# Linear attention and a max-out layer on one core: the k and v projection of batches 3 to 7 moves to the first group spot, into a bank of the down layer

## The chip, the cores and the metric

The kernel runs on one core of one Trainium2 chip. The metric is the device time of one execution, in microseconds (us). Before the change four executions took 328.84, 328.88, 328.73 and 328.17 us, median 328.79. Inside the core five engines run side by side, each in the order of its own instructions: TensorE (PE; its weight loads are listed as PEld), VectorE (DVE), ScalarE (ACT), GpSimd (POOL) and SyncE (SP, which here only issues transfers). They wait for each other with semaphores. PSUM, the memory into which TensorE writes, has eight banks of 512 fp32 columns; what a bank holds must be copied out by VectorE or ScalarE before the bank takes something else.

## The reference

q, k and v are 8 batches x 8 heads x 1024 positions x 64. k and v are first projected from 1024 positions to 64 with E and F; attention over these 64 follows, then a layer of two up matrices, a maximum and a down matrix.

```python
k_proj = np.einsum('ks,bhsd->bhkd', E, k)
v_proj = np.einsum('ks,bhsd->bhkd', F, v)
scores = scale * np.matmul(q, k_proj.transpose(0, 1, 3, 2))
attn = softmax(scores)                       # over the 64 projected positions
x = np.matmul(attn, v_proj)                  # -> 8192 x 512
g = np.maximum(x @ w1, x @ w2)               # 512 -> 1024
out = g @ w_out                              # 1024 -> 512
```

The kernel uses max(a, b) = b + relu(a - b): it forms wd = w1 - w2 and m = w2 @ w_out, so that out = relu(x @ wd) @ w_out + x @ m. Operands are fp16, sums fp32.

## The kernel before

**Units.** The work behind the attention is cut into 16 units, two for each batch (unit n = 2 x batch + half). The up layer (x @ wd with the relu, `up_steps`, matmuls on line 558) and the down layer (`down_steps`, matmuls on line 636) of a unit are each done with seven products instead of eight (Strassen's scheme), from sums and differences of blocks that VectorE makes beforehand (`sums_x`, `sums_g`, line 519). The seven steps come in the order p1, p2, p6, p5, p7, p3, p4. An up step is four matmuls of 128x256, two times over for the two halves of the up layer; a down step is twelve matmuls, cut into three pieces of four.

**Slots.** The order of the work on TensorE is written out by hand in a list of slots. In unit n the down pieces of unit n alternate with the up steps of unit n + 1, and twice in a unit there is a group spot, the slot ("G", n, h). At the group spot the attention is carried on by one group (half the heads, a quarter of a batch): the score matmuls of the next group (line 266), and for the group before it the sums of the exponentials and the products with v (line 278). ScalarE then makes the exponentials (line 355), the logarithm of the sums (line 374) and its inverse (line 377), and VectorE multiplies (line 381). `at_slot` hangs further steps on a slot; they stand behind the slot's own work, in the order in which they were registered.

In an odd unit from 3 on, the first half is: two pieces of the down step p1, the group spot, the third piece of p1 and the first of p2, and then seven up steps with a down piece between each two. The second half has two pieces, the group spot, three pieces, and again seven up steps with pieces between.

**Banks.** Of the eight banks four (0 to 3) carry matmul results (`mm_bank`), and four are two attention tiles of two banks (`att_banks`, two buffers in turn). The up layer and the scores use banks 2 and 3; the down layer uses banks 0 and 1. In an odd unit the down step p1 is in bank 1 and the down step p2 in bank 0, its "second bank"; p6, p7 and p4 reuse the first and p5 and p3 the second. A down or up result that is needed later is copied out by ScalarE (`keep`, line 529); VectorE adds it to a later one (lines 573 and 660). In an even unit the banks 0 and 1 are exchanged, and its last step p4 leaves bank 0 through a ScalarE copy (line 704).

**The projection.** `step_kv` projects k and v of one batch: 8 pairs of matmuls of 512 columns (line 180), k into partitions 0 to 63 and v into 64 to 127 of one bank. For batches 3 to 7 it is hung on the second up step of unit n = 2 x batch - 3, ("U", n, 0, 1), and takes an attention tile. ScalarE copies k out (line 191). VectorE's part is in `finish_v`, which `step_kv` hands back and which is run one slot later: the copy of v (line 196), a doubling of k (line 198), the DMA transpose of k into kpt on SP's queue (line 223), and a copy of v to the other partitions (line 200). The scores of that batch begin at the second group spot of the same unit and need kpt. q of the batch is transposed by two DMAs on SP's queue, hung on the first group spot (line 249). Once kpt is there (`step_gate`, line 229), POOL issues the loads of the next batch's k, v and q.

Of the kernel before, what the change touches and what calls it, by code (L numbers as in the profile page):

```python
# [16 lines left out]
def kernel(  # L17
# [12 lines left out]
    nc = tc.nc  # L30

    B, H, S, D = q.shape
    KP = E.shape[0]
# [26 lines left out]
    def mm_bank(dtype=FP32, n=None):  # L60
        if n is None:
            n = turn.pop(0)
            turn.append(n)
        return ps.tile([128, 512 if dtype == FP32 else 1024], dtype, tag=f"mm{n}", name="mm_ps")

    def att_banks(dtype=FP32):
        return ps.tile(
            [128, 2, 512 if dtype == FP32 else 1024], dtype, tag="att", bufs=2, name="att_ps"
        )
# [53 lines left out]
    for f0, f1 in ((0, 256), (256, 512), (512, DF)):  # L123
        for w_sb, w in ((w2_sb, moe_w2), (w1_sb, moe_w1)):
            for z in range(2):
                nc.gpsimd.dma_start(
                    out=w_sb.rearrange("p (g z) f -> p g z f", z=2)[:, :, z, f0:f1],
                    in_=w.rearrange("(g p z) f -> p g z f", p=128, z=2)[:, :, z, f0:f1],
# [22 lines left out]
    for i in range(2):  # L151
        eft_ps = mm_bank()
        for c in range(NC):
            nc.tensor.transpose(
                out=eft_ps[:, c * KP : (c + 1) * KP],
                in_=ef_v[:, i, c, :],
# [3 lines left out]
        eng = nc.scalar.copy if i else nc.vector.tensor_copy  # L160
# [8 lines left out]
        t["qt"] = qtp.tile([128, H, HALF], FP16, tag="qt", name="qt_sb")  # L169


    def step_kv(t, h0=0, h1=H, which="kv", att=False, dma=False):
        kv_ps = att_banks()[:, 0, :] if att else mm_bank()
        n = (h1 - h0) * D
        both = which == "v"
        for c in range(NC):
            for w in which:
                i = "kv".index(w)
                for r in range(2) if both else (i,):
                    nc.tensor.matmul(  # L180
                        out=kv_ps[r * KP : (r + 1) * KP, 0:n],
                        lhsT=eft[:, i, c, :],
                        rhs=t[w][:, h0:h1, c, :],
                        start=(c == 0), stop=(c == NC - 1),
                    )
        fl = lambda ap: ap[:, h0:h1].rearrange("p h z d -> p (h z d)")
        zd = lambda ap: ap.rearrange("p (h d z) -> p h z d", d=D // 2, z=2)
        if "k" in which:
            eng = nc.vector.tensor_copy if which == "k" else nc.scalar.copy
            kp = t["kp"][:, h0:h1]  # L190
            eng(out=kp[:, :, 0, :], in_=kv_ps[0:KP, 0:n].rearrange("p (h d) -> p h d", d=D))
        if both:
            nc.vector.tensor_copy(out=t["vp"][:, h0:h1], in_=zd(kv_ps[:, 0:n]))
        elif "v" in which:
            def finish_v():
                nc.vector.tensor_copy(out=t["vp"][KP:128, h0:h1], in_=zd(kv_ps[KP:128, 0:n]))
                if dma:
                    nc.vector.tensor_copy(out=kp[:, :, 1, :], in_=kp[:, :, 0, :])
                    step_kpt_dma(t)
                nc.vector.tensor_copy(out=fl(t["vp"][0:KP]), in_=fl(t["vp"][KP:128]))  # L200

            if att:
                return finish_v
            finish_v()
# [17 lines left out]
    def step_kpt_dma(t):  # L222
        nc.sync.dma_start_transpose(
            out=t["kpt"], in_=t["kp"].rearrange("p h r d -> p (h r d)")
        )
# [230 lines left out]
    U = {(b, o): {"n": n, "b": b, "o": o, "t": tiles[b]} for n, (b, o) in enumerate(units)}  # L456
# [260 lines left out]
    t = tiles[0]  # L717
    new_attn(t)
    new_xt(t)
    step_kv(t, 0, 4, "k")  # L720
    warm(2)
    step_kpt(t, 0, 4)
# [5 lines left out]
    step_sc(t, 0, 1)  # L728
    warm(2)
    step_kv(t, 4, 8, "k")  # L730
    step_dn(t, 0, 0)
    warm(2)
# [7 lines left out]
    step_sc(t, 1, 0)  # L740
    step_sc(t, 1, 1)
    step_kv(t, 0, 4, "v")
    step_dn(t, 1, 0)
    step_inv(t, 1, 0)
# [37 lines left out]
    for n, key in enumerate(units):  # L782
        downs = down_steps(U[key], n == last)
        if n in (0, last):
            for p, pieces in enumerate(downs):
                slots += [(("P", n, p, i), x) for i, x in enumerate(pieces)]
            continue
        pieces = [(("P", n, p, i), x) for p, x in enumerate(downs) for i, x in enumerate(x)]
        ups = [*up_steps(U[units[n + 1]])]
        for h, (x, y) in enumerate(((3, 3), (2, 1)) if n == 1 else ((2, 2), (2, 3))):  # L790
            slots += pieces[:x]
            slots.append((("G", n, h), lambda: None))
            slots += pieces[x : x + y]
            del pieces[: x + y]
            for i in range(7):
                slots.append((("U", n, h, i), ups.pop(0)))
                if i < 6:
                    slots.append(pieces.pop(0))
        assert not pieces and not ups
# [3 lines left out]
    def at_slot(key, s, *a):  # L803
        steps.setdefault(key, []).append(lambda: s(*a))
# [11 lines left out]
    t = tiles[1]  # L816
# [26 lines left out]
    t = tiles[2]  # L843
# [8 lines left out]
    for b in range(3, B):  # L852
        t = tiles[b]
        n = 2 * b - 3
        at_slot(("G", n, 0), new_attn, t)
        at_slot(("G", n, 0), step_qt_dma, t, 0, H // 2)
        at_slot(("G", n, 0), step_qt_dma, t, H // 2, H)
        at_slot(("U", n, 0, 1), step_kv, t, 0, H, "kv", True, True)
        at_slot(("U", n, 0, 6), step_gate, t)
        at_slot(("U", n, 0, 6), loads, b + 1, "k", "v", "q")  # L860
    groups = [(tiles[b], g, j) for b in range(1, B) for j in range(2) for g in range(2)][2:]
    none = (None, None, None)
    for i, (new, old) in enumerate(zip([*groups[1:], none], groups)):
        n, h = divmod(i + 2, 2)
# [25 lines left out]
    for key, slot in slots:  # L890
        r = slot()
        pending = [g for g in [r, *(f() for f in pending)] if g is not None]
        for s in steps.pop(key, ()):
            r = s()
# [34 lines left out]
```

## Time and profile before

| | |
|---|---|
| median of four executions | 328.79 us |
| the profiled execution's own time | 328.84 us |
| its span | 327.1 us |
| TensorE busy, granted clock | 317.2 us (97%), 0.999 |
| VectorE busy | 239.6 us (73%) |
| ScalarE busy | 201.1 us (61%) |

The profile shows one execution. Lines of the order of time give start, length, engine, source line, operation, what it writes and reads, and in brackets how long the engine was idle before it and what ended that. Lines of waits give the engine and what it was about to do, whom it waited for, and the total, the number and the longest of these waits. A line number is that of the kernel before.

### The profile page before, as it was taken

What the parts mean: (1) busy time and instruction counts of PE and PEld (TensorE: products, weight loads), DVE (VectorE), ACT (ScalarE), POOL (GpSimd) and SP (SyncE); (2) the same over time, 40 slices, a digit from 0 to 9 for tenths busy, and PEclk for the clock granted to TensorE, in tenths of its full rate; (3) what the DMA queues carried; (4) which work ended last, traced back from release to release, by engine and by line L of the source; (5) the groups of instructions that cost most, each with busy time, mean ns of one, the idle gap of its engine ahead of it and who ended that gap; (6) DMA issues with size and microseconds to landing.
All of it is one profiled execution on the core that took longest, in us unless ns stands there. A gap on an engine that the chain in (4) does not pass through costs nothing.

```text
span 327.1 us, 9015 instructions
## 1 busy us (share of the span) xinstructions
PE 317.2 (97%) x3856; PEld 248.6 (76%) x3856; DVE 239.6 (73%) x424; ACT 201.1 (61%) x359; POOL 37.0 (11%) x56
## 2 busy tenths in 40 slices
PE   8989999999999999999999999999999999999994
PEld 3554547877887788878887888868887888888883
DVE  1355898985968787777967796986967796969572
ACT  2365322566776677667776777656776777765541
POOL 8556002003000210003000300003000000000000
PEclk9999999999999999999999999999999999999999
DMA  8999999978999699996999699877999120212032
GB/s 152 201 199 196 207 208 207 218 171 156 188 236 247 116 165 241 206 179 103 219 199 190 111 196 240 177 156 108 222 206 216 42 99 32 98 34 98 33 130 96
DMA packets 74680, 53.14 MB, mean 162 GB/s; under 512 B 29456, under 2 KB 74512, under 8 KB 74640
## 3 DMA queue, kind: packets, MB, share of 16 engines
q0 software_dynamic: 29376, 28.31, 54.4%
q1 hardware_dynamic: 45264, 24.25, 30.4%
q8 instruction: 30, 0.49, 0.6%
q14 instruction: 10, 0.08, 0.1%
HBM read 57.15 MB, written 16.78 MB: 226 GB/s over the span
## 4 chain that ended last, share of the span: by engine, by line
PE 85%; DMA 9%; DVE 4%; issue 1%; ACT 0%; POOL 0%; DVEq 0%; SPq 0%; POOLq 0%
PE mm_ps L636 43%; PE mm_ps L558 25%; PE att_ps L180 4%; DMA v_sb<-in_v_dram 4%; PE mm_ps L404 4%; PE att_ps L278 3%; PE mm_ps L266 3%; PE mm_ps L440 2%; DMA k_sb<-in_k_dram 2%; DMA big<-in_moe_w_dram 1%; DMA kpt_sb<-kp_sb 1%; DVE o_sb L660 1%; DVE gt_sb L573 1%; DVE xt_sb L329 1%; PE mm_ps L427 1%
## 5 line engine op out<-in xcount | busy, mean ns | idle before, releaser
L529 ACT COPY p_sb<-mm_ps 128x512 f32<-128x512 f32 x172 | 97.1, 594 | 43.0 <-PE mm_ps L558 30.6
L636 PEld LDWEIGHTS <-big 128*128 128x128 f16 x768 | 73.6, 98 | 12.0 <-issue 3.5
L636 PE MATMUL mm_ps<-T_sb,big 128*128 128x256 f16 x576 | 78.0, 273 | 0.0
L573 DVE TENSOR_TENSOR gt_sb<-mm_ps,p_sb 128x512 f16<-128x512 f32 x56 | 38.6, 688 | 46.6 <-PE mm_ps L558 43.4
L558 PE MATMUL mm_ps<-big,big 128*128 128x256 f16 x336 | 50.4, 273 | 0.0
L558 PEld LDWEIGHTS <-big 128*128 128x128 f16 x448 | 43.8, 98 | 5.3 <-issue 0.2
L636 PEld LDWEIGHTS <-gt_sb 128*128 128x128 f16 x384 | 35.7, 98 | 9.7 <-issue 5.4
L636 PE MATMUL mm_ps<-wo_sb,gt_sb 128*128 128x256 f16 x256 | 42.9, 273 | 0.1
L558 PEld LDWEIGHTS <-wd_sb 128*128 128x128 f16 x336 | 32.9, 98 | 4.2 <-issue 0.4
L558 PE MATMUL mm_ps<-xt_sb,wd_sb 128*128 128x256 f16 x224 | 33.6, 273 | 0.2 <-ACT ex_sb L355 0.2
L355 ACT ACTIVATE ex_sb<-mm_ps 128x512 f16<-128x512 f32 x50 | 27.2, 597 | 10.5 <-PE att_ps L278 7.0
L381 DVE TENSOR_TENSOR xt_sb<-att_ps,ld_sb 128x1024 f16<-128x1024 f32 x26 | 31.7, 1219 | 0.1
L660 DVE TENSOR_TENSOR o_sb<-mm_ps,p_sb 128x512 f32<-128x512 f32 x32 | 21.9, 685 | 11.0 <-PE mm_ps L636 7.6
L636 PE MATMUL mm_ps<-m_sb,xt_sb 128*128 128x256 f16 x128 | 24.4, 273 | 0.0
L608 ACT ACTIVATE gt_sb<-mm_ps 128x512 f16<-128x512 f32 x28 | 16.8, 600 | 8.7 <-PE mm_ps L558 8.7
L519 DVE TENSOR_TENSOR big<-gt_sb 128x1024 f16<-128x1024 f16 x32 | 21.9, 685 | 0.2
L576 DVE TENSOR_SCALAR gt_sb<-gt_sb 128x512 f16<-128x512 f16 (+1 forms) x56 | 20.5, 366 | 1.9
L636 PE MATMUL mm_ps<-T_sb,gt_sb 128*128 128x256 f16 x128 | 21.5, 273 | 0.0
L636 PE MATMUL mm_ps<-wo_sb,big 128*128 128x256 f16 x128 | 21.5, 273 | 0.0
L636 PEld LDWEIGHTS <-xt_sb 128*128 128x128 f16 x192 | 18.8, 98 | 2.2
L229 POOL COPY junk<-kpt_sb 1x1 f16<-1x1 f16 x5 | 0.9, 177 | 162.0 <-DMA kpt_sb<-kp_sb 162.0
L573 DVE TENSOR_TENSOR gt_sb<-p_sb 128x512 f16<-128x512 f32 x28 | 19.1, 682 | 0.0
(85 smaller groups left out, 427.9 us busy)
## 6 DMA issues: line engine op xcount, KB each, us to landing
out_dram<-o_sb SPq DMA_DIRECT2D x63, 256.0 KB, 3.0
k_sb<-in_k_dram POOLq DMA_DIRECT2D x7, 1024.0 KB, 10.6
v_sb<-in_v_dram POOLq DMA_DIRECT2D x7, 1024.0 KB, 17.6
q_sb<-in_q_dram POOLq DMA_DIRECT2D x7, 1024.0 KB, 22.2
k_sb<-in_k_dram POOLq DMA_DIRECT2D x4, 256.0 KB, 7.0
q_sb<-in_q_dram POOLq DMA_DIRECT2D x4, 256.0 KB, 8.1
v_sb<-in_v_dram POOLq DMA_DIRECT2D x2, 512.0 KB, 12.2
big<-in_moe_w_dram POOLq DMA_DIRECT2D x8, 128.0 KB, 10.0
```

The source lines that it names most:

```text
L180: nc.tensor.matmul(out=kv_ps[r * KP : (r + 1) * KP, 0:n], lhsT=eft[:, i, c, :], rhs=t[w][:, h0:h1, c, :], start=(c == 0), stop=(c == NC - 1),)
L355: nc.scalar.activation(out=t["ex", g, j][:, e, :], in_=banks[e], func=ACTF.Exp, scale=scale)
L381: nc.vector.tensor_tensor(out=x_out(t, g, j).rearrange("q z o n -> q o z n"), in0=at_ps.rearrange("q o (z n) -> q o z n", z=2), in1=ld[:, ...
L404: nc.tensor.matmul(out=h_ps, lhsT=wd_sb[:, r, fb * 128 : (fb + 1) * 128], rhs=t["xt"][:, r, :, j * W : (j + 1) * W], start=(r == 0), stop= ...
L519: nc.vector.tensor_tensor(out=S(i), in0=x, in1=y, op=op)
L529: copy(out=x, in_=bank)
L558: nc.tensor.matmul(out=bank[:, m * W : (m + 1) * W], lhsT=w_[:, n_, (2 * d + m) * 128 : (2 * d + m + 1) * 128], rhs=a[:, n_, :], start=(n ...
L573: nc.vector.tensor_tensor(out=c_blk(j, c), in0=two(x), in1=two(y), op=ALU.add)
L576: nc.vector.tensor_scalar_max(ap, ap, 0.0)
L608: nc.scalar.activation(out=out, in_=in_, func=ACTF.Relu)
L636: nc.tensor.matmul(out=bank[:, i * CH : (i + 1) * CH], lhsT=a(c)[:, i * 128 : (i + 1) * 128], rhs=w_(c), start=(n is not None and m == (lo ...
L660: nc.vector.tensor_tensor(out=o_sb, in0=two(x), in1=two(y), op=ALU.add)
```

## The change

For batches 3 to 7 the projection is hung on the first group spot of the unit, ahead of the group's own matmuls, and goes into bank 0, the bank of the down step p2. Both copies out of it are made by VectorE, and with them the doubling, the transpose and the second copy of v come at once and not a slot later. In every odd unit from 3 on (13 too, which has no projection) one down piece moves from ahead of the first up step to the second half, so that each down piece of the first half from p2's first on stands one up step later. Units 1 and the even ones keep their order.

```diff
-    def step_kv(t, h0=0, h1=H, which="kv", att=False, dma=False):
-        kv_ps = att_banks()[:, 0, :] if att else mm_bank()
-        n = (h1 - h0) * D
+    def step_kv(t, h0=0, h1=H, which="kv", att=False, dma=False, n=None):
+        kv_ps = att_banks()[:, 0, :] if att else mm_bank(n=n)
+        size = (h1 - h0) * D
...
         if "k" in which:
-            eng = nc.vector.tensor_copy if which == "k" else nc.scalar.copy
+            eng = nc.vector.tensor_copy if which == "k" or n is not None else nc.scalar.copy
             kp = t["kp"][:, h0:h1]
...
-        for h, (x, y) in enumerate(((3, 3), (2, 1)) if n == 1 else ((2, 2), (2, 3))):
+        for h, (x, y) in enumerate(((3, 3), (2, 1)) if n == 1 else ((2, 1), (3, 3)) if n % 2 else ((2, 2), (2, 3))):
             slots += pieces[:x]
             slots.append((("G", n, h), lambda: None))
...
         at_slot(("G", n, 0), step_qt_dma, t, H // 2, H)
-        at_slot(("U", n, 0, 1), step_kv, t, 0, H, "kv", True, True)
+        at_slot(("G", n, 0), step_kv, t, 0, H, "kv", False, True, 0)
         at_slot(("U", n, 0, 6), step_gate, t)
```

The remaining lines of the diff only write `size` where `n` stood.

## The prediction

> **What bounds the kernel now.** I read the page's busy shares first, then TensorE's waits after the load phase, then the order of time around the place where the change works.
>
> ```profile
> PE 317.2 (97%) x3856; PEld 248.6 (76%) x3856; DVE 239.6 (73%) x424; ACT 201.1 (61%) x359; POOL 37.0 (11%) x56
> ```
>
> TensorE is busy 97% of the span. What stops it after the first 60 us is short; this is the whole list of its waits from 60 us to the end:
>
> ```profile
> PE mm_ps L266 <- DMA kpt_sb<-kp_sb: 0.9, 1, 0.9
> PE mm_ps L558 <- ACT ex_sb L355: 0.2, 1, 0.2
> ```
>
> So from 60 us on TensorE's order is the time: the change can win at most the 0.9 us wait, or gaps between its instructions, and each new wait of TensorE is lost time. Order of time in the first half of unit 9, where batch 6 is projected (start us, length, engine, line):
>
> ```profile
> 208.23 0.58 ACT L704 COPY o_sb<-mm_ps 128x512 f32<-128x512 f32 x1 [0.72 <-PE mm_ps L636]
> ...
> 209.31 5.57 SPq L249 DMA_TRANSPOSE qt_sb<-q_sb  x2
> ...
> 209.43 0.41 PE L266 MATMUL mm_ps<-qt_sb,kpt_sb 64*32 64x256 f16 x16
> ...
> 210.11 0.39 PE L636 MATMUL mm_ps<-wo_sb,gt_sb 128*128 128x256 f16 x2
> ...
> 211.37 0.68 DVE L519 TENSOR_TENSOR big<-big,gt_sb 128x1024 f16<-128x1024 f16 x1
> ...
> 212.39 1.44 PEld L180 LDWEIGHTS <-eft 128*64 128x64 f16 x16 [0.21 <-issue]
> ...
> 213.93 0.38 PE L180 MATMUL att_ps<-v_sb,eft 128*64 128x512 f16 x1
> ...
> 214.25 0.39 PE L636 MATMUL mm_ps<-wo_sb,gt_sb 128*128 128x256 f16 x2
> ...
> 214.38 0.58 ACT L191 CAST kp_sb<-att_ps 64x512 f16<-64x512 f32 x1 [1.42 <-PE att_ps L180]
> ...
> 214.89 0.69 DVE L660 TENSOR_TENSOR o_sb<-mm_ps,p_sb 128x512 f32<-128x512 f32 x1 [1.30 <-PE mm_ps L636]
> ...
> 215.62 0.69 DVE L196 CAST vp_sb<-att_ps 64x512 f16<-64x512 f32 x1
> ...
> 216.34 0.28 DVE L198 COPY kp_sb<-kp_sb 64x512 f16<-64x512 f16 x1
> ...
> 216.78 1.20 SPq L223 DMA_TRANSPOSE kpt_sb<-kp_sb  x1
> ...
> 218.81 0.68 DVE L519 TENSOR_TENSOR big<-gt_sb,big 128x1024 f16<-128x1024 f16 x1
> ...
> 219.40 0.68 DVE L573 TENSOR_TENSOR gt_sb<-mm_ps,p_sb 128x512 f16<-128x512 f32 x1
> ...
> 221.04 0.41 PE L266 MATMUL mm_ps<-qt_sb,kpt_sb 64*32 64x256 f16 x16 [0.93 <-DMA kpt_sb<-kp_sb]
> ```
>
> Four things are to be seen. (1) The k, v projection (L180) holds TensorE from 212.39 to 214.25, 1.86 us. (2) Its copies end late: ACT copies k at 214.38, VectorE does v at 215.62 and the double of k at 216.34, and the transpose to kpt is issued at 216.78; this time it took 4.2 us to land, and the score at 221.04 waited 0.93 us. The other four batches' kpt transposes took 2.7 to 2.8 us, and no wait. (3) VectorE is the engine with a backlog at the group spot: from 204.37 on its instructions follow each other without idle time, and the last of them, the L519 of 211.37, starts 1.94 us after the group's first matmul. (4) Call that first matmul S = 209.43. Units 3, 5 and 7 show that L519 at the same distance (101.90 to 103.82, 137.74 to 139.67, 173.59 to 175.52: 1.92 to 1.93 us).
>
> **The change part by part.**
>
> *TensorE, moved.* The 16 projection matmuls go from behind the second up step to S itself, ahead of the group. Bank 0, which they take, was last read by the L704 copy, 208.23 to 208.81, so they start at S. k and v are in place: batch 4's v was issued at 113.55 and took 17.6 us, to 131.2, and would be needed at 137.74; batch 3's at 80.03 plus 17.5, against 101.90. New order with the durations of before: projection S to S+1.86; group 0.68 (209.43 to 210.11), so the third piece of down step p1 at S+2.54; a piece or an up step is four matmuls, 0.437 us (210.55, 210.99, 211.43 in the trace); so up step p1 at S+2.98, and the first piece of down step p2 at S+3.41. Its bank is the projection's, so it needs both copies out. Up step p1 needs the first exponential out of bank 2: in before that starts 0.47 us after the group's first matmul (209.90) and takes 0.597 us, so S+2.93 with the shift; 0.05 us of room and nothing lost beyond that.
>
> *TensorE, removed.* The array changes shape when it goes to the 64-column projection and back; the gaps are 0.09 us in (last 128x128 matmul at 212.19, next 0.20 later, against 0.11 in a stream) and 0.10 us out (213.93 plus a pair's 0.215 is 214.15, next at 214.25). With the projection directly ahead of the group one of four such gaps goes: 0.10 us for each of five units.
>
> *VectorE, added.* The k copy joins VectorE, behind the four L519 that keep it busy, and the v copy follows. L519 at S+1.94; the next instruction that reads PSUM after an L519 starts 0.59 us later (218.81 to 219.40): k copy at S+2.53. Its data are there at S+1.99 (212.39 to the copy at 214.38), so VectorE is the later. A 64x512 cast on VectorE from PSUM for k is not in the trace: its bounds are 0.416 (the 64x256 cast of the start) and 0.752 us (the longest 64-partition copy of 512 columns in any row, L200); I take 0.694, the v copy of the same size. The v copy then starts 0.60 us (L573, 218.81's successor at 219.40 and the next at 220.00) or 0.72 us (L660 to the v copy, 214.89 to 215.62, and the v copy to the next, 215.62 to 216.34) after the k copy; I take 0.72, since those rows hold this very instruction: S+3.25, end S+3.94.
>
> The Trainium skill has a rule on just this ("VectorE: DVE Perf Modes", section "Two Vector instructions with no wait between them"): an instruction whose operands start in another 32-partition group than the last ones did is held until the earlier ones have finished. The v copy starts at partition 64 and the k copy at 0, so by the rule it is held, and the sum below stands; if it were not held, the sum would be 0.6 us less, 329.9. The trace agrees wherever I looked: 0.72 us around the v copy, 0.60 between two L660 or two L573 of the same length.
>
> *TensorE, the new wait.* A released matmul starts 0.05 us after the end of what it waited for (an exponential from 77.57 for 0.60, the matmul at 78.22). So down step p2 starts at S+3.99 rather than S+3.41: a wait of 0.58 us. Behind it in TensorE's order stand up steps p2 and p6 and the rest of the unit, and nothing later gives it back, as TensorE has no idle time to shrink. Less the 0.10 gap: +0.48 for a unit, x5 = +2.40.
>
> *If that wait were not there*, the next would show: the third up step, p6, reuses bank 2, whose copy (the second L529) ends 3.02 us after the group's first matmul (282.02 to 285.04 in unit 13), S+4.88, ready S+4.93, against an arrival at S+3.41 + 3 x 0.437 = S+4.72: 0.21 us. So the floor is +0.11 for a unit, not -0.10.
>
> *Unit 13* gets the new order of slots without a projection. There p6 would arrive at 282.02 + 0.68 + 5 x 0.437 = 284.89, the copy ends at 285.04, ready 285.09: +0.20, once.
>
> ```profile
> 283.94 1.10 ACT L529 COPY p_sb<-mm_ps 128x512 f32<-128x512 f32 x2
> ...
> 285.33 0.60 PE L558 MATMUL mm_ps<-big,big 128*128 128x256 f16 x4
> ```
>
> *ACT, removed*: 5 x 0.578 us of k copies; ACT stood idle 1.42 us before that of 214.38, so TensorE gains nothing from it. The attention banks lose one tenant for each unit; TensorE never waited for them after 60 us: zero.
>
> *SP and the transposes.* The kpt transpose moves ahead of one output store. It is ready when k is doubled, at S+3.94 + 0.03 + 0.29 = S+4.26, but SP is still issuing the two qt transposes until 214.88 (S+5.45; S+6.72 in unit 3 by 102.63 plus 5.99). So it is issued 0.7 to 1.9 us earlier than before (109.34, 216.78). The score comes at S+10.5 plus 0.48; even 4.2 us from S+5.45, or 4.2 from S+6.72, ends by S+10.92: the 0.93 us wait goes. Behind it, it may queue on the qt transposes still in flight; bounds 2.7 and 4.2 us, which I just used. The store that it passes waits for nothing that TensorE needs; its buffer is one of four.
>
> *POOL*: the gate waits for kpt, and behind it stand the next batch's k, v and q loads, now some 1 us earlier. They have over 4 us in hand: zero.
>
> *VectorE, later.* The L573 of up step p2 comes 0.71 us after that step's start (211.86 to 212.57), so S+5.14, and frees bank 3 at S+5.83; up step p5 needs it at S+3.99 + 5 x 0.437 = S+6.17. Behind it L576 (0.29), L381 (1.22) and L660 (0.69) end at S+8.0; bank 0's next piece comes after seven up steps, at S+9.2. Both hold, by 0.3 and 1.2 us.
>
> **Sum.** +2.40 + 0.20 - 0.93 = +1.67 on the profiled execution's 328.84 (span 327.1), which is 0.05 above the median of 328.79: 330.5.
>
> **The rivals.**
> A. VectorE's queue sets down step p2 (above): 330.5. For: the backlog is at the same place in all five units. With the shortest k copy (0.416) and the v copy's earlier start a unit's +0.48 falls below the floor of 0.11: 328.84 + 0.55 + 0.20 - 0.93 = 328.7; with the longest (0.752) it is 0.54: 330.8.
> B. The copies are short enough that wait and gain cancel: those lower ends, 328.7 to 329.4, no change. Against: rows of this very size.
> C. The other side: the copies come in time, and the 0.93 us wait and five gaps are all that remains: 328.84 - 0.93 - 0.50 = 327.4. It decides if VectorE reaches the k copy at S+1.95, 0.58 us earlier than its queue ended in before, and if ACT frees bank 2 0.21 us earlier too. Against: nothing upstream of that queue changes.
> D. The kpt wait stays or comes back in other units, as the transpose now runs beside those of qt: 330.5 + 0.93 = 331.4, more if twice.
>
> **How the numbers follow.** A 0.66, B 0.13, C 0.08, D 0.13. A measurement of this kernel can tell about 0.2%, 0.66 us, from no change: 328.13 to 329.45 is "same". A and D are slower (0.79, less 0.01 for the low end of A, which is same), B same, C faster. The likeliest case's own range is 329.9 to 331.0; the one for 8 in 10 goes from B's middle to a little past D: 328.9 to 331.7.
>
> **What would show it.** Right: TensorE's waits list mm_ps L636 behind VectorE's vp_sb L196, five times, 0.5 to 0.6 us each; one wait of L558 for p_sb L529 of about 0.2 us in unit 13; no wait for kpt; VectorE's L191 64x512 at 0.69 us; the units of the projections 0.4 to 0.5 us longer. Wrong: that wait absent or under 0.3 us (B, C), or a wait for kpt still in the list (D). I would be wrong above all if VectorE's backlog at S were shorter than I read it.

## The result, and the profile after

| | before | after |
|---|---|---|
| median | 328.96 us (73 runs, 327.65 to 331.76) | 330.28 us (47 runs, 329.0 to 331.3) |
| ratio after to before, beside each other | | 1.0031, 95% interval 1.0021 to 1.0040 |
| one profiled execution, its own time | 328.84 us | 330.43 us |
| its span | 327.1 us | 328.7 us |
| period between two projection units | 35.84 us | 36.10 us |
| unit 13, its first group spot to the last matmul | 40.26 us | 40.45 us |

The ratio, of executions taken beside each other, is a loss of 1.0 us (0.7 to 1.3); the two medians lie 1.3 us apart. The period is the distance between the first group spots of two odd units with a projection (before 101.90, 137.74, 173.59, 209.43; after 102.95, 139.05, 175.15, 211.25, 247.35, 283.45, which is 36.10 five times). Before, one more period holds the kpt wait and is 36.75.

The page's first line of the kernel after, the busy shares:

```profile
PE 316.7 (96%) x3856; PEld 248.9 (76%) x3856; DVE 241.9 (74%) x429; ACT 198.2 (60%) x354; POOL 37.2 (11%) x56
```

TensorE does the same work (3856 instructions as before) and ScalarE's five k copies have gone to VectorE (424 to 429). TensorE's list of waits from 60 us to the end, kernel after (what it was about to do, whom it waited for, total, times, longest):

```profile
PE mm_ps L636 <- DVE vp_sb L196: 2.1, 5, 0.4
PE mm_ps L558 <- ACT ex_sb L355: 0.2, 1, 0.2
```

The wait for kpt is gone, and the down layer waits five times for VectorE's copy of v, as forecast, though the list gives 0.42 us each and not 0.58. Order of time in unit 9 of the kernel after, whose projection starts at S = 211.25 (start us, length, engine, line, operation):

```profile
211.25 1.44 PEld L180 LDWEIGHTS <-eft 128*64 128x64 f16 x16 [0.21 <-issue]
...
213.10 0.41 PE L266 MATMUL mm_ps<-qt_sb,kpt_sb 64*32 64x256 f16 x16
213.18 0.69 DVE L519 TENSOR_TENSOR big<-big,gt_sb 128x1024 f16<-128x1024 f16 x1
...
213.78 0.68 DVE L191 CAST kp_sb<-mm_ps 64x512 f16<-64x512 f32 x1
...
214.22 0.60 PE L558 MATMUL mm_ps<-xt_sb,wd_sb 128*128 128x256 f16 x4
214.49 0.69 DVE L196 CAST vp_sb<-mm_ps 64x512 f16<-64x512 f32 x1
...
215.24 0.60 PE L636 MATMUL mm_ps<-wo_sb,gt_sb 128*128 128x256 f16 x4 [0.42 <-DVE vp_sb L196]
...
216.49 1.79 SPq L223 DMA_TRANSPOSE kpt_sb<-kp_sb  x1
...
222.22 0.40 PE L266 MATMUL mm_ps<-qt_sb,kpt_sb 64*32 64x256 f16 x16
```

Read from the top, this is the forecast's path: VectorE's last L519 at S+1.93 (forecast 1.94), the k copy at S+2.53 (2.53), the v copy at S+3.24 (3.25), the up step p1 at S+2.97 (2.98), the down step p2 at S+3.99 (3.99). The wait that is lost is 215.24 less 214.22 less the 0.437 us of an up step: 0.58 us. The list shows 0.42 of it because it reckons TensorE as busy until the modelled end of the up step (0.60 us long, where the next step follows 0.437 after it in a stream). In unit 13 of the kernel after:

```profile
283.45 0.41 PE L266 MATMUL mm_ps<-qt_sb,kpt_sb 64*32 64x256 f16 x16
...
285.37 1.10 ACT L529 COPY p_sb<-mm_ps 128x512 f32<-128x512 f32 x2
...
286.51 0.60 PE L558 MATMUL mm_ps<-big,big 128*128 128x256 f16 x4
```

The third up step starts 3.06 us after the group's first matmul, 0.04 us after the L529 pair ends. In a stream it would have come after 2.87 us (0.68 for the group and five steps of 0.437), so 0.19 us is lost (forecast 0.20). This wait is not in the list at all; it too lies under a modelled end.

So each forecast wait is there, at its place and with its size, and yet the kernel lost 1.0 us where the sum said 1.7. By the sum the period should have grown by 0.48; it grew by 0.26.

### The profile page after: what moved, and what is told of

Its sections match the earlier page's. It is cut to its first block, busy times and chain, and to the rows that moved or that the text cites. A ratio compares the mean times of both kernels' runs of the same rounds, so it can differ in the third digit from the quotient of the medians.

```text
span 328.7 us, 9012 instructions
## 1 busy us (share of the span) xinstructions
PE 316.7 (96%) x3856; PEld 248.9 (76%) x3856; DVE 241.9 (74%) x429; ACT 198.2 (60%) x354; POOL 37.2 (11%) x56
## 4 chain that ended last, share of the span: by engine, by line
PE 65%; DVE 14%; DMA 13%; issue 3%; POOL 2%; ACT 0%; DVEq 0%; POOLq 0%
PE mm_ps L636 38%; PE mm_ps L558 22%; DMA q_sb<-in_q_dram 8%; DMA v_sb<-in_v_dram 4%; DVE gt_sb L573 4%; DVE big L519 3%; PE att_ps L278 3%; DVE o_sb L660 2%; DVE xt_sb L381 2%; PE mm_ps L266 2%; DMA big<-in_moe_w_dram 2%; DVE vp_sb L196 1%; DVE kp_sb L191 1%; POOL q_sb L102 1%; DVE gt_sb L576 1%
## 5 line engine op out<-in xcount | busy, mean ns | idle before, releaser
L529 ACT COPY p_sb<-mm_ps 128x512 f32<-128x512 f32 x172 | 97.7, 593 | 50.2 <-PE mm_ps L558 31.2
L636 PE MATMUL mm_ps<-T_sb,big 128*128 128x256 f16 x576 | 77.0, 273 | 0.0
L573 DVE TENSOR_TENSOR gt_sb<-mm_ps,p_sb 128x512 f16<-128x512 f32 x56 | 38.6, 690 | 51.5 <-PE mm_ps L558 47.2
L660 DVE TENSOR_TENSOR o_sb<-mm_ps,p_sb 128x512 f32<-128x512 f32 x32 | 21.9, 683 | 4.5 <-ACT p_sb L529 3.5
L519 DVE TENSOR_TENSOR big<-gt_sb 128x1024 f16<-128x1024 f16 x32 | 21.9, 684 | 0.1
L573 DVE TENSOR_TENSOR gt_sb<-p_sb 128x512 f16<-128x512 f32 x28 | 19.1, 683 | 0.0
```

The lines of the kernel that those rows point to most:

```text
L519: nc.vector.tensor_tensor(out=S(i), in0=x, in1=y, op=op)
L529: copy(out=x, in_=bank)
L573: nc.vector.tensor_tensor(out=c_blk(j, c), in0=two(x), in1=two(y), op=ALU.add)
L636: nc.tensor.matmul(out=bank[:, i * CH : (i + 1) * CH], lhsT=a(c)[:, i * 128 : (i + 1) * 128], rhs=w_(c), start=(n is not None and m == (lo ...
L660: nc.vector.tensor_tensor(out=o_sb, in0=two(x), in1=two(y), op=ALU.add)
```

## The experiments

**Theory one**: the copies on VectorE cost what was forecast (+0.48 a period), and the new order of slots gives 0.22 us back, from a wait that the kernel before has at its second group spot and that no list of waits shows. **Its rival**: the order of slots only costs, and the 0.22 us comes from the moved projection itself. For the loss there are rivals too: VectorE's backlog ahead of the copies, the shared bank as such, or the transpose. Order of time around the second group spot of unit 7, kernel before:

```profile
183.56 0.68 DVE L573 TENSOR_TENSOR gt_sb<-mm_ps,p_sb 128x512 f16<-128x512 f32 x1
...
183.74 0.30 PE L278 MATMUL att_ps<-ex_sb,ones 64*32 64x256 f16 x8
...
184.08 0.62 PE L266 MATMUL mm_ps<-qt_sb,kpt_sb 64*32 64x256 f16 x16
...
184.30 0.13 PEld L266 LDWEIGHTS <-kpt_sb 64*32 64x32 f16 x13 [0.23 <-issue]
...
184.63 1.49 PE L636 MATMUL mm_ps<-T_sb,big 128*128 128x256 f16 x12
```

and the kernel after:

```profile
183.77 0.69 DVE L573 TENSOR_TENSOR gt_sb<-mm_ps,p_sb 128x512 f16<-128x512 f32 x1
...
185.78 0.30 PE L278 MATMUL att_ps<-ex_sb,ones 64*32 64x256 f16 x8
...
186.01 0.23 PEld L266 LDWEIGHTS <-kpt_sb 64*32 64x32 f16 x16
...
186.12 0.40 PE L266 MATMUL mm_ps<-qt_sb,kpt_sb 64*32 64x256 f16 x16
...
186.45 1.48 PE L636 MATMUL mm_ps<-T_sb,big 128*128 128x256 f16 x12
```

From the group's first matmul to the down piece behind it there are 0.89 us before and 0.67 after. The 16 score matmuls (L266) take 0.62 instead of 0.40. They go in pairs into banks 2 and 3 in turn, and in before VectorE's L573 still reads bank 3, until 184.24. The row of the weight loads (PEld) shows where TensorE stops: after the third load it is idle for 0.23 us, and the other 13 loads start at 184.30, 0.06 us after L573 has ended; the third score matmul, the first into bank 3, starts there too. In after bank 3 is free 1.7 us ahead of the scores, and the 16 loads are one row. In the matmuls' own rows a wait between matmuls of one row makes the row longer, and the list of waits has no entry for it.

**1. The new order of slots alone**, without the moved projection (a diff against before):

```diff
-        for h, (x, y) in enumerate(((3, 3), (2, 1)) if n == 1 else ((2, 2), (2, 3))):
+        for h, (x, y) in enumerate(((3, 3), (2, 1)) if n == 1 else ((2, 1), (3, 3)) if n % 2 else ((2, 2), (2, 3))):
```

> The kernel before with the new order of slots in the odd units alone: the projection stays behind the second up step, in its attention tile, its k copied by ScalarE. The trace of the change shows 36.10 us from one projection unit to the next where the prediction had 0.48 over 35.84, so 0.22 us less. Theory one: the 0.22 is a wait in the second group spot that the list of waits does not show, the score matmuls of 0.62 us (0.40 to 0.41 where they run through) that wait in their middle for bank 3, which VectorE's L573 frees late; one more piece ahead of the second group lets L573 finish, so the period goes to 35.62 and the score matmuls to 0.40. Unit 13 loses 0.19 us. With the kpt wait of before (0 to 0.93 us) gone as well, 0.9 to 1.8 us faster than before, about 327.5. Theory two: the 0.22 is a larger gap at the switch of the array's shape, which this kernel leaves as in before: the period stays at 35.84, and the time is 0.2 slower to 0.7 us faster. Under both no wait of TensorE for a copy of the projection.

327.92 us, ratio 0.9964 (0.9942 to 0.9985): faster than before. The period is 35.63, unit 13's stretch 40.44. Its second group spot in unit 7:

```profile
182.61 0.68 DVE L573 TENSOR_TENSOR gt_sb<-mm_ps,p_sb 128x512 f16<-128x512 f32 x1
...
183.96 0.30 PE L278 MATMUL att_ps<-ex_sb,ones 64*32 64x256 f16 x8
...
184.29 0.40 PE L266 MATMUL mm_ps<-qt_sb,kpt_sb 64*32 64x256 f16 x16
...
184.63 1.48 PE L636 MATMUL mm_ps<-T_sb,big 128*128 128x256 f16 x12
```

One piece more ahead of the second group puts VectorE's L573 well in front of the scores, and the group takes 0.67 us again. The order alone is worth 0.21 us a period; the rival falls.

**2. The moved projection alone**, with the order of slots of before (a diff against after):

```diff
-        for h, (x, y) in enumerate(((3, 3), (2, 1)) if n == 1 else ((2, 1), (3, 3)) if n % 2 else ((2, 2), (2, 3))):
+        for h, (x, y) in enumerate(((3, 3), (2, 1)) if n == 1 else ((2, 2), (2, 3))):
```

> The change without its new order of slots: the projection at the first group spot, in bank 0, copied by VectorE, and the first piece of down step p2 ahead of the first up step. If VectorE's queue sets the release of bank 0, that is 3.99 us after the first projection matmul whatever comes between, and p2's first piece stands 2.98 us after it: TensorE waits 1.0 us in each of five units, the period grows by 0.92 us over before less what the second group spot gives back (0.22 if the hidden wait there goes, as VectorE is done with the projection earlier): 36.5 to 36.8. Unit 13 as in before. In all 3.0 to 4.6 us slower than before. The rival, that the copies by themselves are late and not the queue ahead of them, expects the same here.

332.39 us, ratio 1.0091 (1.0067 to 1.0116), period 36.55. Its list of waits from 60 us on:

```profile
PE mm_ps L636 <- DVE vp_sb L196: 4.3, 5, 0.9
PE mm_ps L558 <- ACT ex_sb L355: 0.2, 1, 0.2
```

Without the later place of p2 the same wait is one step (0.44 us) longer. 0.58 + 0.44 less the 0.10 of the gap would be +0.92 a period; measured is +0.71. The 0.21 us between them is the hidden wait again: here too the scores of the second group take 0.40 us (unit 9, at 223.19), since TensorE now comes later to them while VectorE does not: L573 starts 9.9 us after the first matmul of the first group spot (10.0 in unit 7 of before), the scores 11.4 us after it (10.5). So in these kernels what holds TensorE back ahead of that group spot is repaid there, up to 0.22 us.

**3. The k copy given back to ScalarE** (against after), which leaves VectorE only the v copy:

```diff
-            eng = nc.vector.tensor_copy if which == "k" or n is not None else nc.scalar.copy
+            eng = nc.vector.tensor_copy if which == "k" else nc.scalar.copy
```

> The change with the k copy given back to ScalarE. If VectorE's queue and two copies in a row set the wait, then ScalarE copies k at 1.99 to 2.57 us after the first projection matmul, VectorE's v copy ends at 3.3, and the wait of down step p2 for it goes (arrival 3.4). But the exponentials then start 0.2 us later on ScalarE, and the first up step waits for bank 2 (about 0.2 us) and the third up step for the second copy of ScalarE (about 0.3 us): the period 35.95 to 36.05 against 36.10, so 0.2 to 0.8 us faster than the change and 0.2 to 0.8 slower than before. The rival, that ScalarE has room to spare in this place, expects the wait simply gone: the period 35.5 to 35.6, 1 us faster than before or more.

328.65 us, ratio 0.9983 (0.9963 to 1.0002), period 35.83. Unit 9, projection at S = 211.34:

```profile
213.33 0.58 ACT L191 CAST kp_sb<-mm_ps 64x512 f16<-64x512 f32 x1 [2.10 <-PE mm_ps L180]
...
213.81 1.07 ACT L355 ACTIVATE ex_sb<-mm_ps 128x512 f16<-128x512 f32 x2
...
213.99 0.69 DVE L196 CAST vp_sb<-mm_ps 64x512 f16<-64x512 f32 x1
...
214.45 0.60 PE L558 MATMUL mm_ps<-xt_sb,wd_sb 128*128 128x256 f16 x4
...
215.25 1.07 ACT L529 COPY p_sb<-mm_ps 128x512 f32<-128x512 f32 x2
...
216.37 0.60 PE L558 MATMUL mm_ps<-big,big 128*128 128x256 f16 x4
```

The wait for L196 is gone from the list, so the second copy in VectorE's queue, not the bank as such, made it. In its place ScalarE is late: the up step p1 comes at S+3.11 (0.13 late) and the third up step at S+5.03 (0.31 late, the 0.13 within it). The expected period of 35.95 to 36.05 was too high. It fits the sum of both waits (35.52 + 0.2 + 0.3 = 36.02), but the first lies within the second; and the first is only 0.13, as ScalarE's exponential started 0.48 us after the k copy, though that copy's row is 0.58 long. So the time is not 0.2 to 0.8 us above before as expected but 0.6 below by the ratio, with an interval that just takes in no change.

**4. VectorE's backlog moved behind the copies** (against after): two of the four L519 ahead of the k copy are run later.

```diff
             where = tuple((("U", n - 2, 1, k), i) for k, i in ((6, 2), (3, 0), (4, 1), (5, 3)))
+            if n - 1 in (3, 5, 7, 9, 11):
+                where = ((("P", n - 1, 0, 2), 2), *where[1:])
...
-            for key, i in (end, 0), (("P", n, 0, 0), 1), (("P", n, 1, m), 2), (("P", n, 2, m), 3):
+            for key, i in (end, 0), (("P", n, 0, 2 if n in (3, 5, 7, 9, 11) else 0), 1), (("P", n, 1, m), 2), (("P", n, 2, m), 3):
```

> The change with two of VectorE's four L519 (one sum of x, one of g) moved from ahead of the projection's copies to behind them; everything else as in the change. Theory: the backlog is the cause, so the k copy starts when its data are there, 1.99 us after the first projection matmul and not 2.53, the v copy ends at 3.40 and down step p2 starts at 3.45 against an arrival of 3.41: TensorE's wait falls from 0.58 to under 0.1 us. What shows next is the third up step's wait for ScalarE's copy, about 0.2 us. Period 35.65 to 35.80 against 36.10, so 1.5 to 2.2 us faster than the change, and 0.5 to 1.3 us faster than before. Rival: two copies in series on one engine are too long by themselves; the wait stays at 0.4 us or more and the time within 0.5 us of the change.

327.98 us, ratio 0.9972 (0.9954 to 0.9990), period 35.78. Unit 9, projection at S = 209.30:

```profile
211.29 0.68 DVE L191 CAST kp_sb<-mm_ps 64x512 f16<-64x512 f32 x1 [0.31 <-PE mm_ps L180]
...
212.00 0.69 DVE L196 CAST vp_sb<-mm_ps 64x512 f16<-64x512 f32 x1
...
212.75 0.60 PE L636 MATMUL mm_ps<-wo_sb,gt_sb 128*128 128x256 f16 x4
...
213.07 1.10 ACT L529 COPY p_sb<-mm_ps 128x512 f32<-128x512 f32 x2
...
214.22 0.60 PE L558 MATMUL mm_ps<-big,big 128*128 128x256 f16 x4
```

The copies have the same engine, bank and length, and only start 0.54 us earlier after S. The down step p2 now comes at S+3.45, and the loss of the kernel after is a gain. So the two copies in a row and the shared bank fit by themselves, and the backlog ahead of them made the loss; with one copy less (experiment 3) even the backlog fits. Next in line is the wait that the prediction named as the floor: the third up step at S+4.92 (forecast ready at S+4.93, arrival S+4.72).

**5. The new order, but not in unit 13** (against before):

```diff
-        for h, (x, y) in enumerate(((3, 3), (2, 1)) if n == 1 else ((2, 2), (2, 3))):
+        for h, (x, y) in enumerate(((3, 3), (2, 1)) if n == 1 else ((2, 1), (3, 3)) if n in (3, 5, 7, 9, 11) else ((2, 2), (2, 3))):
```

> The new order of slots on the kernel before, as in the run of the order alone, but for units 3 to 11 only; unit 13 keeps the old order. If the 0.19 us of unit 13 are the third up step's wait for ScalarE's copy, they go: from unit 13's group spot to the last matmul 40.26 us as in before, not 40.44, the period 35.62 as with the order alone, and no wait for kpt. About 1.1 us and the wait for kpt less than before: 327.3 to 327.9. If unit 13's loss came from elsewhere (a later engine at the end), it stays at 40.44.

327.62 us, ratio 0.9949 (0.9921 to 0.9976), period 35.63, unit 13's stretch 40.25 against 40.44 in experiment 1. The order costs 0.19 us in unit 13, whose second group spot has no scores, so no hidden wait pays for it there.

**6. All that helped together** (a diff against experiment 4: the group spot of units 3 to 11 stands one piece earlier, and unit 13 is as before):

```diff
-        for h, (x, y) in enumerate(((3, 3), (2, 1)) if n == 1 else ((2, 1), (3, 3)) if n % 2 else ((2, 2), (2, 3))):
+        for h, (x, y) in enumerate(((3, 3), (2, 1)) if n == 1 else ((1, 2), (3, 3)) if n in (3, 5, 7, 9, 11) else ((2, 2), (2, 3))):
```

> What the change could be with its waits out of the way: the projection at the first group spot in bank 0 and copied by VectorE as in the change, two of VectorE's L519 behind the copies, unit 13 in its old order, and the group spot one piece earlier (one piece ahead of it and two behind it, three and three in the second half) so that the first up step again comes two pieces after the group. Expected: down step p2 3.85 us after the first projection matmul, the copies done at 3.45; the third up step at 5.16, ScalarE's copy ready at 4.93: no wait at either. The gap at one switch of the array's shape (0.10) is saved on top of the 0.22 of the second group spot: period 35.52 against 35.84 of before and 36.10 of the change. In all 1.6 us and the wait for kpt less than before: 326.8 to 327.4, the fastest. Rival: the projection's place costs something that the waits do not show, and the period is 35.62 or more, as with the order alone.

327.29 us, ratio 0.9932 (0.9908 to 0.9957), period 35.52, unit 13's stretch 40.25. It is the fastest of all that ran, 2.2 us below before by the ratio and 1.5 by the medians (328.83 beside it), though its interval overlaps with that of experiment 5. Unit 9, projection at S = 209.01:

```profile
212.78 1.10 ACT L529 COPY p_sb<-mm_ps 128x512 f32<-128x512 f32 x2
...
212.85 0.60 PE L636 MATMUL mm_ps<-wo_sb,gt_sb 128*128 128x256 f16 x4
...
214.16 0.60 PE L558 MATMUL mm_ps<-big,big 128*128 128x256 f16 x4
```

With one piece fewer ahead of the group spot and one more behind it, p2 and every up step stand 0.44 us later after the projection: p2 at S+3.84, the third up step at S+5.15, 0.28 us after the L529 pair has ended. So neither waits. Against experiment 5 its period is 0.10 us shorter: the one change of the array's shape that the moved projection saves, now to be had.

**7. The transpose alone** (against before, TensorE's order untouched): the v copy, the doubling and the kpt transpose come in the projection's own slot, ahead of L660.

```diff
-            if att:
+            if att and not dma:
                 return finish_v
```

> The kernel before, with VectorE's part of the projection (v copy, doubling of k, transpose to kpt, second v copy) issued ahead of the down sum L660 and not behind it; TensorE's order is the same. The transpose to kpt is issued 0.7 to 0.8 us earlier, VectorE is done with its list some 0.1 us later. It prices the wait for kpt by itself: with landings of 2.7 to 4.2 us the longest wait falls from 0.93 to 0.2 us, the period stays at 35.8 to 35.95. If the wait for kpt costs the kernel before half a microsecond on average, this is 0.3 to 0.6 us faster than before; if the profiled 0.93 was a rare case, it is within 0.2 us.

327.98 us, ratio 0.9971 (0.9950 to 0.9991), period 35.73. Unit 9:

```profile
214.33 0.69 DVE L196 CAST vp_sb<-att_ps 64x512 f16<-64x512 f32 x1 [1.40 <-ACT kp_sb L191]
...
215.50 1.19 SPq L223 DMA_TRANSPOSE kpt_sb<-kp_sb  x1
...
215.69 0.69 DVE L660 TENSOR_TENSOR o_sb<-mm_ps,p_sb 128x512 f32<-128x512 f32 x1
...
218.64 0.68 DVE L573 TENSOR_TENSOR gt_sb<-mm_ps,p_sb 128x512 f16<-128x512 f32 x1
...
219.27 0.51 PE L266 MATMUL mm_ps<-qt_sb,kpt_sb 64*32 64x256 f16 x16
```

kpt is issued 6.7 us after the first group spot instead of 7.35, and no wait for it is left. The period fell further than the expected 35.8 to 35.95: the scores of the second group take 0.49 to 0.51 us where they took 0.62, so half of the hidden wait goes with it, because L573 moves up in VectorE's queue as well (9.86 us after the first group spot, 9.97 in unit 7 of before). So the run does not price the wait for kpt by itself: of its 0.95 us by the ratio the period accounts for 0.55, and the 0.4 left is uncertain by 0.7.

**What the seven give together.** The terms, each from a row named above, against the period of 35.84 of before:

| | terms | worked out | measured |
|---|---|---|---|
| after | -0.10 gap, -0.22 hidden wait, +0.58 p2 | 36.10 | 36.10 |
| 1 and 5, order | -0.22 | 35.62 | 35.63 |
| 2, move alone | -0.10, -0.22, +1.02 p2 | 36.54 | 36.55 |
| 3, k by ScalarE | -0.10, -0.22, +0.31 third up step | 35.83 | 35.83 |
| 4, backlog later | -0.10, -0.22, +0.20 third up step, +0.06 fourth (at 215.15, just after VectorE's L573 of 214.41 ends, where 215.09 would be in a stream) | 35.78 | 35.78 |
| 6, all | -0.10, -0.22 | 35.52 | 35.52 |
| 7, transpose | -0.11 | 35.73 | 35.73 |

## Why the prediction was right, and where its sum was off

- **What sets the new wait**: right in the place, the cause and the size (0.58 us, five times). Experiments 3 and 4 each took away one half of the cause, a copy or the backlog, and the wait went. The Trainium skill's rule ("VectorE: DVE Perf Modes", section "Two Vector instructions with no wait between them") agrees with the rows: the v copy, which starts at another partition than the k copy, came 0.71 us after it (213.78 to 214.49), and the k copy 0.60 us after an L519 of the same length (213.18 to 213.78).
- **The gap of 0.10 us and unit 13's 0.20 us**: right. Experiment 6 against 5 shows the first alone, experiment 5 against 1 the second (0.19).
- **"Nothing later gives it back, as TensorE has no idle time to shrink"**: this step was wrong. TensorE had 0.22 us to shrink at the second group spot of each unit with a projection (0.62 us rows at 112.39, 148.24, 184.08 and 256.67 in before; in unit 9 the kpt wait lay over it), inside the rows of the scores, where neither the busy share of 97% nor the list of waits shows it; only the weight loads' idle time does. The unit's term was +0.48 and measured +0.26; five times 0.22 is 1.1 us of the sum.
- **"Less 0.93 for the kpt wait"**: right that it goes (no kernel with an earlier transpose shows it), but taken from one execution as if each one had it. The ratio of after says +1.02; its trace terms are 5 x 0.26 + 0.19 = +1.49, so the wait's removal was worth some 0.5 us. By the same reckoning experiments 1 to 7 give 0.3, 0.6, 0.7, 0.8, 0.6, 0.6 and 0.4 (number 6: 0.0068 x 328.8 is 2.24, less 5 x 0.32). Each is uncertain by 0.3 to 0.9, they share executions of before, and by the medians in place of the ratios the mean is nearer 0.3. That the average is below 0.9 is argued from this, not shown.
- **The sum**: +1.67 forecast, where the ratio says +1.0. Two errors partly cancel in it, which is luck: the 0.22 us that is given back in each unit made it 1.1 too high, and the kpt wait at its full 0.93 made it some 0.5 too low. The two profiled executions do differ by +1.6, and that is luck too. In it are +1.05 us before the first changed instruction: batch 1's projection starts at 48.53 in before and at 49.58 in after. In the nine profiles, of kernels that are the same up to there, that start lies anywhere from 48.10 to 50.38. With the five periods, unit 13 and the kpt wait of that one execution, 1.05 + 1.30 + 0.19 - 0.91 is 1.63. The median of 330.28 lies only 0.2 below the forecast of 330.5 because the medians differ by 1.3 us where the ratio says 1.0, and because before's own median, over more executions, is 328.96 and not 328.79.
- **The transposes**: the forecast bounds of 2.7 and 4.2 us for kpt held nearly: in after the five took 3.4 at the median and 4.4 at most. Landing was never late, so rival D fell. The cover that I named for it (SP's queue busy with qt) was there: in after kpt was issued at S+4.6 to S+5.9, in unit 9 0.11 us after the qt issue ended (211.13 plus 5.25).
- **Rivals B and C** fell as forecast. The first condition of C holds up: when VectorE is ready for the k copy before its data are (0.31 us of idle time ahead of it at S+1.99 in experiment 4), the kernel is faster than before, by 0.9 us and not C's 1.4, as the third up step still waits for ScalarE (C's second condition). B's short copies were not there: the k copy took 0.68.
- **What the profile would show**: five L196 waits, as said, but 0.4 us in the list for 0.58 lost, and unit 13's 0.2 us not in it. I had read the list as if it gave whole losses. The units of the projections grew by 0.26 us and not by 0.4 to 0.5.

## What to carry to other kernels

Before saying that a bound engine has nothing to shrink, compare the length of like groups of small instructions along the span: one that takes 0.62 us here and 0.40 there hides a wait that the list of waits lacks, and a delay put ahead of it costs that much less. When a copy is moved to another engine, look at what stands in that engine's queue at the time rather than at its busy share; here VectorE was busy 73%, and two instructions moved out of the way turned a loss of 1.0 us into a gain. And a wait seen once among five of its kind is worth its average over executions, not its size in the one profile.

## What was not expected of the hardware

- A matmul's modelled end hides the start of a wait: 0.42 us listed for 0.58 lost, and 0.19 lost with none listed (kernel after, units 9 and 13).
- The load phase scatters: the same instructions reached the same point between 48.10 and 50.38 us in nine profiles.
- A kpt transpose took 2.7 to 2.9 us in experiments 1, 5 and 7 (in before four times 2.7 to 2.8, once 4.2), and 2.8 to 4.6 us in the kernels with the moved projection, where it is issued 0.1 to 0.2 us behind those of qt. What makes the difference is not shown: in experiment 1 one was issued at 108.99, 0.1 us behind qt's issue and before qt landed at 110.94, and took 2.8 us.
- ScalarE started the next instruction 0.48 us after a 64x512 copy from PSUM whose row is 0.58 us long (213.33 and 213.81 in experiment 3).
